# Gated linear attention with a squared-ReLU FFN: attention stages dealt into equal parts of FFN groups of four blocks, products of one shape kept together, loads issued from two queues

## The chip, the core and the metric

The kernel runs on one core of one Trainium2 chip. Its engines have a queue each and run side by side: TensorE (PE: matmuls; PEld: the loading of their stationary operand), VectorE (DVE), ScalarE (ACT), GpSimd (POOL) and SyncE (SP), which issues transfers. The metric is the device time of one execution in microseconds, as the median of several runs.

## What is computed

For each of 4 batches and 8 heads of width 48, over 768 positions, a state of 48 x 48 decays by alpha per row and takes up the outer product of k and v; q reads it. The result, 3072 tokens of 384, goes through an FFN with a hidden width of 2048. The weights of the FFN come as 64-bit floats, all else as 32-bit.

```python
for t in range(S):
    state = alpha[:, :, t, :, None] * state + np.einsum('bhd,bhe->bhde', k[:, :, t], v[:, :, t])
    y[:, :, t] = np.einsum('bhd,bhde->bhe', q[:, :, t], state)
...
h = np.maximum(x @ w_in, 0.0)
return (h * h @ w_out).astype(np.float32)
```

## The kernel before

A block is one batch and one chunk of 128 positions, all eight heads; block n is chunk n // 4 of batch n % 4, so there are 24, and the first four (chunk 0) have no state yet. Two heads make a pair: each head has 64 partitions, 48 of its own and 16 of padding. A block passes four stages:

- `decays` (line 190): alpha is turned on PE (aT), ACT takes Ln (la), DVE adds up along the chunk (the scan of line 195), ACT takes two Exp (b and inv).
- `turn` (206): q and k are turned on PE and scaled by b and inv on DVE.
- `scores` (215): sc, the products of k and q, two heads side by side in the rows of the array; DVE copies their causal part to am (226); k is turned back (kr) and copied by ACT to ks, but not in the last chunk.
- `values` (238): kv, the new part of the state (250), added by DVE in sm (259 or 261) and decayed by POOL (278); then y. For each of four pairs of heads y takes a full product with the old state (267, all 128 columns of the array; not at chunk 0) and two column-half ones, one for each head, of am with v (271). ACT copies y to yg and to xT. Heads have 48 rows and the FFN wants 128 full ones, so the fourth pair's rows fill the padding of the other three: six DMAs from yg to xT on SP (291).

The FFN works on groups of blocks, GROUPS = [2, 2, 4, 4, 4, 4, 4]. `ffn_in(g, j)` (299) makes 128 of the hidden rows for all columns of the group (h, three matmuls, 512 columns for four blocks), ACT's relu (r, line 313) and DVE's square (hid, line 314); `ffn_out(g, t, i)` (318) adds an eighth of the hidden rows to block t's output (o), and at the last eighth copies it and sends it out. A 32-bit matmul shows as two MATMUL instructions in the trace, a transpose as one. h and r have two buffers each.

The weights come in 16 pieces, eight of w_in and then eight of w_out, 768 KB each. `load_weights` (99) brings a piece to a raw buffer, of which there are two; a w_in piece takes four DMAs, all on SP. `convert_weights` (116) makes 32-bit floats of it: one ACT operation (129), five on DVE (130 to 145), two on POOL (148, 149). `next_weights` (157) converts the next piece and starts one more load.

The order of the work is written out by hand and each engine keeps it. The loop of line 357 turns block n, takes the decays of block n + 1, the values of block n - 1 and the scores of block n, with `ffn(0.25, n)` behind each: `next_weights`, then as many FFN units as make a quarter of a block's work. A group's units are queued once the values of its last block are issued, so that its first h stands right behind that y on PE. Conversion starts with block 0.

Of the kernel before, what the change touches and what calls it, by code (L numbers as in the profile page):

```python
# [15 lines left out]
GROUPS = [2, 2, 4, 4, 4, 4, 4]  # L16
# [3 lines left out]
def kernel(  # L20
# [32 lines left out]
    assert S % C == 0 and H * D == DM and NP == KM + 1 and KM * G == D and sum(GROUPS) == NBLK  # L53
# [6 lines left out]
    p3 = ctx.enter_context(tc.tile_pool(name="p3", bufs=3))  # L60
    x_pool = ctx.enter_context(tc.tile_pool(name="x", bufs=3))
# [12 lines left out]
    tiles["v"] = kept("v_in", NV, [128, H, 64])  # L74
    for i in range(NV):
        for x, value in (("a", 1.0), ("q", 0.0), ("k", 0.0), ("v", 0.0)):
            if i < len(tiles[x]):
                nc.gpsimd.memset(tiles[x][i][:, :, D:64], value)
# [7 lines left out]
    def load(n):  # L86
        c, b = divmod(n, B)
        for x in "aqkv":
            nc.sync.dma_start(  # L89
                out=tiles[x][n % len(tiles[x])][:, :, 0:D],  # L90
                in_=srcs[x][b, :, c * C : (c + 1) * C, :].rearrange("h s d -> s h d"),
            )
# [6 lines left out]
    def load_weights(i):  # L99
        dst = (w_in + w_out)[i]  # L100
        dt = moe_w_in.dtype
        raw = dst if dt == FP32 else raw_pool.tile(list(dst.shape), dt, tag="raw", name="raw")
        raws[i] = raw
        if i < NW:
            src = moe_w_in[:, i * DF // NW : (i + 1) * DF // NW]
            own = src[0 : 2 * KM * D].rearrange("(k e r) f -> e r k f", e=2, r=D)
            gap = src[2 * KM * D : DM].rearrange("(e k r) f -> e r k f", e=2, r=G)
# [70 lines left out]
    blk_group = [(g, t) for g, m in enumerate(GROUPS) for t in range(m)]  # L178
# [11 lines left out]
    def decays(n):  # L190
        ps = turned("a", n)
        la = p2.tile([128, NP, C], FP32, tag="la", name="la")
        nc.scalar.activation(out=la, in_=ps, func=AF.Ln)  # L193

        nc.vector.tensor_tensor_scan(  # L195
            out=la.rearrange("a p t -> a (p t)"),
            data0=again.rearrange("a p t -> a (p t)"),
            data1=la.rearrange("a p t -> a (p t)"),
            initial=0.0, op0=ALU.mult, op1=ALU.add,
        )  # L200
        b = bs[n] = p3.tile([128, NP, C], FP32, tag="b", name="b")
        nc.scalar.activation(out=b, in_=la, func=AF.Exp)
        inv = invs[n] = p2.tile([128, NP, C], FP32, tag="inv", name="inv")
        nc.scalar.activation(out=inv, in_=la, func=AF.Exp, scale=-1.0)

    def turn(n):
        qkT[n] = []
        for x, factor in (("q", bs[n]), ("k", invs.pop(n))):
            ps = turned(x, n)
            t = (p3 if x == "q" else p2).tile([128, NP, C], FP32, tag=f"{x}T", name=f"{x}T")  # L210
            nc.vector.tensor_tensor(out=t, in0=ps, in1=factor, op=ALU.mult)  # L211
            qkT[n].append(t)

    def scores(n):
        qT, kT = qkT[n]
        ps = [ps_att.tile([128, NP, C], FP32, tag="att", name="sc") for _ in range(2)]
        for p in range(NP):
            for e in range(2):
                rows = slice(64 * e, 64 * e + 64)
                nc.tensor.matmul(  # L220
                    out=ps[e][:, p, :], lhsT=kT[rows, p, :], rhs=qT[rows, p, :],
                    start=True, stop=True,
                )
# [14 lines left out]
    def values(n):  # L238
# [7 lines left out]
        if c < NCH - 1:  # L246
            kv = ps_att.tile([128, NP, C], FP32, tag="att", name="kv")
            kt = ks.pop(n)
            for p in range(NP):
                nc.tensor.matmul(  # L250
                    out=kv[:, p, :], lhsT=kt[:, p, :],
                    rhs=v_in[:, 2 * p : 2 * p + 2, :].rearrange("a h d -> a (h d)"),
                    start=True, stop=True,
                )
            sm = p2.tile([128, NP, D], FP32, tag="sm", name="sm")
            for e in range(2):
                rows, cols = slice(64 * e, 64 * e + 64), slice(64 * e, 64 * e + D)
                if c == 0:
                    nc.vector.tensor_copy(out=sm[rows], in_=kv[rows, :, cols])
                else:  # L260
                    nc.vector.tensor_tensor(
                        out=sm[rows], in0=kv[rows, :, cols], in1=st[rows, :, cols], op=ALU.add
                    )
        y = ps_att.tile([128, NP, C], FP32, tag="att", name="y")
        for p in range(NP):
            if c:
                nc.tensor.matmul(  # L267
                    out=y[:, p, :], lhsT=st[:, p, :], rhs=qT[:, p, :], start=True, stop=False
                )
            for e in range(2):  # L270
                nc.tensor.matmul(  # L271
                    out=y[64 * e : 64 * e + 64, p, :], lhsT=v_in[:, 2 * p + e, :],
                    rhs=am[:, e, p, :], start=(c == 0), stop=True,
                )
        if kv is not None:
            for e in range(2):
                rows, cols = slice(64 * e, 64 * e + 64), slice(64 * e, 64 * e + D)
                nc.gpsimd.tensor_tensor(  # L278
                    out=st[rows, :, cols], in0=sm[rows],
                    in1=b[rows, :, C - 1 : C].to_broadcast([64, NP, D]), op=ALU.mult,  # L280
                )
        g, t = blk_group[n]
        if t == 0:
            xT[g] = x_pool.tile([128, KM, 512], FP32, tag="xT", name="xT")
# [14 lines left out]
    def ffn_in(g, j):  # L299
        n = GROUPS[g] * C  # L300
        hid[g, j] = hid_pool.tile([128, 512], FP32, tag="hid", name="hid")
        w, c0 = w_in[j * NW // NJ], j % (NJ // NW) * 128
        ps = ps_h.tile([128, 512], FP32, tag="h", name="h")
        for kk in range(KM):
            nc.tensor.matmul(  # L305
                out=ps[:, 0:n],
                lhsT=w[:, kk, c0 : c0 + 128],
                rhs=xT[g][:, kk, 0:n],
                start=(kk == 0),
                stop=(kk == KM - 1),  # L310
            )
        r = p2.tile([128, 512], FP32, tag="r", name="r")
        nc.scalar.activation(out=r[:, 0:n], in_=ps[:, 0:n], func=AF.Relu)  # L313
        nc.vector.tensor_tensor(  # L314
            out=hid[g, j][:, 0:n], in0=r[:, 0:n], in1=r[:, 0:n], op=ALU.mult
        )

    def ffn_out(g, t, i):
        per = NJ // NW
        if i == 0:  # L320
            acc[g, t] = ps_o.tile([128, 512], FP32, tag="o", name="o")
        ps = acc[g, t]
        for j in range(per):
            nc.tensor.matmul(  # L324
                out=ps[:, 0:DM],
                lhsT=hid[g, per * i + j][:, t * C : (t + 1) * C],
                rhs=w_out[i][:, j, :],
                start=(i == 0 and j == 0),
                stop=(i == NW - 1 and j == per - 1),
            )  # L330
        if i == NW - 1:
            o = p2.tile([128, DM], FP32, tag="osb", name="osb")
            nc.scalar.activation(out=o, in_=acc.pop((g, t))[:, 0:DM], func=AF.Copy)  # L333
            c, b = divmod(sum(GROUPS[:g]) + t, B)
# [4 lines left out]
    units = []  # L339
    behind = [0.0]  # L340

    def add_group(g):
        m = GROUPS[g]
        units.extend((KM * m * C, ffn_in, (g, j)) for j in range(NJ))
        units.extend((NJ // NW * DM, ffn_out, (g, t, i)) for t in range(m) for i in range(NW))

    def ffn(share, n):
        next_weights()
        behind[0] = behind[0] + share * C * NJ * KM * 2 if units else 0.0
        while units and behind[0] > 0:  # L350
            cost, fn, args = units.pop(0)
            behind[0] -= cost
            fn(*args)

    load(2)
    decays(0)
    for n in range(NBLK + 1):
        if n < NBLK:
            turn(n)
        ffn(0.25, n)  # L360
        if n + 1 < NBLK:
            decays(n + 1)
        ffn(0.25, n)
        if n:
            values(n - 1)
            g, t = blk_group[n - 1]
            if t == GROUPS[g] - 1:
                add_group(g)
        if n + 3 < NBLK:
            load(n + 3)  # L370
        ffn(0.25, n)
        if n < NBLK:
            scores(n)
        ffn(0.25, n)
    while units:
        _, fn, args = units.pop(0)
        fn(*args)
# [30 lines left out]
```

## Time and profile before

| | |
|---|---|
| median of 3 runs | 795.09 us (794.25 to 796.36) |
| the profiled execution | 797.68 us |
| its span | 795.9 us |
| its granted TensorE clock, mean | 0.929 |
| PE busy | 684.4 us (86%) |
| DVE busy | 262.8 us (33%) |
| ACT busy | 153.2 us (19%) |
| POOL busy | 87.5 us (11%) |
| DMA, mean over the span | 48 GB/s |

The profile is of one execution. Line numbers are those of the kernel before; tiles go by the names in the code. In the chain of work a row is a start, a length, an engine or a DMA, and what it did; rows of it say what the last instruction of the kernel was waiting for at that time. In the timelines a row is an operation, with its output, its inputs, their sizes and how many were merged, and in brackets how long the engine sat idle before it and what ended that. In the groups by line stand the busy time, the mean in nanoseconds of one, and the idle time before them with its cause.

### The profile page before, as it was taken

To read this page: it belongs to the slowest core of one execution; us is meant where nothing else is said; L and a number is where in the kernel's file an instruction comes from. 1 tells how busy PE (TensorE), PEld (TensorE's weight loads), DVE (VectorE), ACT (ScalarE), POOL (GpSimd) and SP (SyncE) were. 2 spreads that over 40 slices of the span, in tenths; PEclk is the share of its full clock that TensorE was granted. 3 is DMA by queue.
4 is the path that set the end of the run, shared out by engine and by line. 5 is a ranking of instruction groups with operands and counts; after the bars stand their busy time and mean duration, and the time that the engine had idled before them with its cause. 6 is when DMAs were issued, how large, how long until landed. Compare 5 with 4: busy or idle time off the path is not lost.

```text
span 795.9 us, 7515 instructions
## 1 busy us (share of the span) xinstructions
PE 684.4 (86%) x2896; PEld 411.7 (52%) x2896; DVE 262.8 (33%) x360; ACT 153.2 (19%) x293; POOL 87.5 (11%) x93
## 2 busy tenths in 40 slices
PE   4132487779996999997999998999989999979998
PEld 3132365467673556663456654556654456644454
DVE  5589899123141342111341112341113331002200
ACT  2121233123031231111230111220111220012100
POOL 3455634100010000000000000000000000000000
PEclk9555599889998999999999998999998999999999
DMA  9986624030235023123023203023302000000000
GB/s 155 166 141 143 154 80 82 11 53 0 53 55 82 1 42 53 25 47 43 2 41 53 50 23 43 7 36 53 52 21 41 4 2 11 23 13 1 0 21 20
DMA packets 113699, 37.85 MB, mean 48 GB/s; under 512 B 103168, under 2 KB 108544, under 8 KB 113664
## 3 DMA queue, kind: packets, MB, share of 16 engines
q1 hardware_dynamic: 113664, 37.37, 27.2%
q8 instruction: 23, 0.38, 0.2%
q14 instruction: 12, 0.10, 0.0%
HBM read 31.46 MB, written 4.72 MB: 45 GB/s over the span
## 4 chain that ended last, share of the span: by engine, by line
PE 80%; DMA 6%; DVE 6%; SPq 5%; issue 1%; ACT 1%; POOL 0%; ACTq 0%; DVEq 0%; POOLq 0%
PE h L305 32%; PE o L324 31%; PE y L271 4%; PE y L267 4%; DMA raw<-in_moe_w_in_dram 3%; PE sc L220 3%; SPq L89 2%; PE kv L250 2%; DMA xT<-yg 2%; SPq L291 1%; PE kr L234 1%; PE qT L185 1%; PE kT L185 1%; PE aT L185 1%; DVE cut L133 1%
## 5 line engine op out<-in xcount | busy, mean ns | idle before, releaser
L305 PE MATMUL h<-xT,w_in 128*128 128x512 f32 (+1 forms) x672 | 273.0, 562 | 52.7 <-DMA xT<-yg 40.6
L324 PE MATMUL o<-w_out,hid 128*128 128x384 f32 x768 | 256.9, 490 | 5.7 <-POOL w_out L149 5.7
L305 PEld LDWEIGHTS h<-xT,w_in 128*128 128x128 f32 x672 | 132.3, 203 | 168.8 <-issue 141.7
L324 PEld LDWEIGHTS o<-w_out,hid 128*128 128x128 f32 x768 | 143.3, 191 | 100.7 <-POOL w_out L149 6.8
L314 DVE TENSOR_TENSOR hid<-r 128x512 f32<-128x512 f32 (+1 forms) x112 | 78.9, 712 | 251.3 <-ACT r L313 251.3
L313 ACT ACTIVATE r<-h 128x512 f32<-128x512 f32 (+1 forms) x112 | 59.6, 534 | 233.9 <-PE h L305 222.2
L278 POOL TENSOR_TENSOR s<-sm,b 64x192 f32<-64x192 f32 x40 | 22.4, 560 | 434.2 <-PE y L267 415.3
L226 DVE COPY_PREDICATED am<-causal,sc 128x512 f32<-128x512 uint32 x48 | 32.3, 727 | 93.2 <-PE sc L220 93.0
L271 PE MATMUL y<-am,v_in 128*64 128x128 f32 x384 | 41.3, 307 | 8.3 <-DVE qT L211 8.3
L195 DVE TENSOR_TENSOR_SCAN la<-again,la 128x512 f32<-128x512 f32 x24 | 29.3, 1220 | 43.2 <-ACT la L193 43.1
L333 ACT ACTIVATE osb<-o 128x384 f32<-128x384 f32 x24 | 11.8, 490 | 141.8 <-PE o L324 130.6
L267 PE MATMUL y<-qT,s 128*128 128x128 f32 x160 | 37.0, 313 | 0.0
L220 PEld LDWEIGHTS sc<-qT,kT 64*128 64x128 f32 x384 | 25.4, 198 | 14.9 <-issue 11.6
L211 DVE TENSOR_TENSOR qT<-qT,b 128x512 f32<-128x512 f32 x24 | 16.4, 685 | 47.0 <-PE qT L185 31.5
L220 PE MATMUL sc<-qT,kT 64*128 64x128 f32 x384 | 30.5, 298 | 1.4 <-ACT la L193 1.4
L185 PE MATMUL aT<-ident,a_in 128*128 128x128 f32 x96 | 16.5, 300 | 17.5 <-DMA a_in<-in_alpha_dram 10.2
L271 PEld LDWEIGHTS y<-am,v_in 128*64 128x64 f32 x384 | 20.7, 142 | 18.8 <-DVE qT L211 8.8
L267 PEld LDWEIGHTS y<-qT,s 128*128 128x128 f32 x160 | 24.2, 189 | 11.8 <-issue 11.2
L185 PE MATMUL kT<-ident,k_in 128*128 128x128 f32 x96 | 16.1, 295 | 14.6 <-ACT ks L236 14.5
L185 PEld LDWEIGHTS aT<-ident,a_in 128*128 128x128 f32 x96 | 12.7, 154 | 25.7 <-DVE am L226 8.1
L250 PEld LDWEIGHTS kv<-v_in,ks 128*128 128x128 f32 x160 | 22.4, 206 | 5.1 <-DVE hid L314 1.4
L193 ACT ACTIVATE la<-aT 128x512 f32<-128x512 f32 x24 | 14.3, 595 | 54.3 <-PE aT L185 54.3
(42 smaller groups left out, 343.0 us busy)
## 6 DMA issues: line engine op xcount, KB each, us to landing
raw<-in_moe_w_out_dram SPq DMA_DIRECT2D x8, 768.0 KB, 4.5
a_in<-in_alpha_dram SPq DMA_DIRECT2D x24, 192.0 KB, 3.4
q_in<-in_q_dram SPq DMA_DIRECT2D x24, 192.0 KB, 3.9
k_in<-in_k_dram SPq DMA_DIRECT2D x24, 192.0 KB, 4.5
v_in<-in_v_dram SPq DMA_DIRECT2D x24, 192.0 KB, 4.7
raw<-in_moe_w_in_dram SPq DMA_DIRECT2D x16, 288.0 KB, 6.4
out_dram<-osb SPq DMA_DIRECT2D x24, 192.0 KB, 1.9
xT<-yg SPq DMA_DIRECT2D x144, 8.0 KB, 1.7
```

The source lines that it names most:

```text
L185: nc.tensor.transpose(out=ps[:, p, :], in_=rows[:, 128 * p : 128 * (p + 1)], identity=ident)
L195: nc.vector.tensor_tensor_scan(out=la.rearrange("a p t -> a (p t)"), data0=again.rearrange("a p t -> a (p t)"), data1=la.rearrange("a p t ...
L220: nc.tensor.matmul(out=ps[e][:, p, :], lhsT=kT[rows, p, :], rhs=qT[rows, p, :], start=True, stop=True,)
L226: nc.vector.copy_predicated(out=am_t[n % NAM][:, e], mask=causal.bitcast(U32).unsqueeze(1).to_broadcast([128, NP, C]), data=ps[e],)
L250: nc.tensor.matmul(out=kv[:, p, :], lhsT=kt[:, p, :], rhs=v_in[:, 2 * p : 2 * p + 2, :].rearrange("a h d -> a (h d)"), start=True, stop=True,)
L267: nc.tensor.matmul(out=y[:, p, :], lhsT=st[:, p, :], rhs=qT[:, p, :], start=True, stop=False)
L271: nc.tensor.matmul(out=y[64 * e : 64 * e + 64, p, :], lhsT=v_in[:, 2 * p + e, :], rhs=am[:, e, p, :], start=(c == 0), stop=True,)
L278: nc.gpsimd.tensor_tensor(out=st[rows, :, cols], in0=sm[rows], in1=b[rows, :, C - 1 : C].to_broadcast([64, NP, D]), op=ALU.mult,)
L305: nc.tensor.matmul(out=ps[:, 0:n], lhsT=w[:, kk, c0 : c0 + 128], rhs=xT[g][:, kk, 0:n], start=(kk == 0), stop=(kk == KM - 1),)
L313: nc.scalar.activation(out=r[:, 0:n], in_=ps[:, 0:n], func=AF.Relu)
L314: nc.vector.tensor_tensor(out=hid[g, j][:, 0:n], in0=r[:, 0:n], in1=r[:, 0:n], op=ALU.mult)
L324: nc.tensor.matmul(out=ps[:, 0:DM], lhsT=hid[g, per * i + j][:, t * C : (t + 1) * C], rhs=w_out[i][:, j, :], start=(i == 0 and j == 0), st ...
```

## The change

The groups are six of four blocks (GB = 4). Before the first FFN unit all four blocks of the first group pass their attention stages; then a group's FFN is cut into 16 equal slots, and ahead of each slot stands one stage of a block of the next group: slot 0 decays of its first block, slot 1 turn, slot 2 scores, slot 3 values, and so on to slot 15. A slot holds two `ffn_in` (slots 0 to 7) or four `ffn_out`. Conversion begins with block 3, three pieces before slot 0, then one piece in even slots and two in odd ones. Inputs of three blocks are loaded at the start, ahead of all weights; there are three raw buffers; the lower half of each w_in piece is loaded by SP and the upper half by ACT. In y all full products come first and all column-half ones after them. v lies without padding, so that kv has 96 columns instead of 128 and sc, sm and the decay of the state use 48 rows for a head instead of 64. b, q's and xT's tiles lose a buffer each.

```diff
-GROUPS = [2, 2, 4, 4, 4, 4, 4]
+GB = 4
...
-    raw_pool = ctx.enter_context(tc.tile_pool(name="raw", bufs=2))
+    raw_pool = ctx.enter_context(tc.tile_pool(name="raw", bufs=NR))
...
-    p3 = ctx.enter_context(tc.tile_pool(name="p3", bufs=3))
-    x_pool = ctx.enter_context(tc.tile_pool(name="x", bufs=3))
+    x_pool = ctx.enter_context(tc.tile_pool(name="x", bufs=2))
...
+    tiles["v"] = kept("v_in", NV, [128, H * D + G])
...
-            for e in range(2):
-                nc.sync.dma_start(out=raw[64 * e : 64 * e + D], in_=own[e])
-                nc.sync.dma_start(out=raw[64 * e + D : 64 * e + 64], in_=gap[e])
+            for e, dma in enumerate((nc.sync, nc.scalar)):
+                dma.dma_start(out=raw[64 * e : 64 * e + D], in_=own[:, e])
+                dma.dma_start(out=raw[64 * e + D : 64 * e + 64], in_=gap[:, e])
...
-    load(0)
-    load_weights(0)
-    load(1)
-    load_weights(1)
-    to_load, to_convert = list(range(2, 2 * NW)), list(range(2 * NW))
+    for n in range(NIN):
+        load(n)
+    to_load, to_convert = list(range(2 * NW)), list(range(2 * NW))
...
-                rows = slice(64 * e, 64 * e + 64)
+                rows = slice(64 * e, 64 * e + D)
...
-                    rhs=v_in[:, 2 * p : 2 * p + 2, :].rearrange("a h d -> a (h d)"),
-                    start=True, stop=True,
+                    rhs=v_in[:, 2 * p * D : 2 * (p + 1) * D], start=True, stop=True,
...
+        if c:
+            for p in range(NP):
+                nc.tensor.matmul(
+                    out=y[:, p, :], lhsT=st[:, p, :], rhs=qT[:, p, :],
+                    start=(p == 0), stop=False, skip_group_check=True,
+                )
         for p in range(NP):
-            if c:
-                nc.tensor.matmul(
-                    out=y[:, p, :], lhsT=st[:, p, :], rhs=qT[:, p, :], start=True, stop=False
-                )
             for e in range(2):
                 nc.tensor.matmul(
-                    out=y[64 * e : 64 * e + 64, p, :], lhsT=v_in[:, 2 * p + e, :],
-                    rhs=am[:, e, p, :], start=(c == 0), stop=True,
+                    out=y[64 * e : 64 * e + 64, p, :], lhsT=v_in[:, (2 * p + e) * D : (2 * p + e) * D + 64],
+                    rhs=am[:, e, p, :], start=(c == 0 and p == 0), stop=True,
+                    skip_group_check=True,
                 )
...
+    stages = [decays, turn, scores, values]
+    order = [(0, 0), (0, 1), (1, 0), (0, 2), (1, 1)]
+    for n in range(2, GB):
+        order += [(n - 2, 3), (n, 0), (n - 1, 2), (n, 1)]
+    order += [(GB - 2, 3), (GB - 1, 2), (GB - 1, 3)]
+    for n, s in order:
+        stages[s](n)
+        if s == 1 and n + NIN < GB:
+            load(n + NIN)
+            for _ in range(2):
+                load_weights(to_load.pop(0))
+        if s == 3 and n + NV == GB:
+            load(n + NV)
+            load_weights(to_load.pop(0))
+        if n == GB - 1 and s > 0:
+            next_weights()
+
+    NS = GB * len(stages)
+    for g in range(NBLK // GB):
+        units = [(ffn_in, (g, j)) for j in range(NJ)]
+        units += [(ffn_out, (g, t, i)) for t in range(GB) for i in range(NW)]
+        cost = {ffn_in: KM * GB * C, ffn_out: NJ // NW * DM}
+        total = sum(cost[f] for f, _ in units)
+        done = 0
+        for slot in range(NS):
+            i, s = divmod(slot, len(stages))
+            n = (g + 1) * GB + i
+            if n < NBLK:
+                stages[s](n)
+            for _ in range(1 + s % 2):
+                next_weights()
+            if s == 0 and n + 1 < NBLK:
+                load(n + 1)
+            while units and done * NS < total * (slot + 1):
+                f, args = units.pop(0)
+                f(*args)
+                done += cost[f]
```

PE before, around the end of a group of four: o belongs to the group that ends, h to the next, kv and y to the block whose columns complete it.

```order
L324 MATMUL o<-w_out_136,hid 128x384 x2
L250 MATMUL kv<-v_in_99,ks 128x128 x4
L267 MATMUL y<-qT,s_116 128x128
L271 MATMUL y<-am_170,v_in_99 64x128 x2
L267 MATMUL y<-qT,s_116 128x128
L271 MATMUL y<-am_170,v_in_99 64x128 x2
L267 MATMUL y<-qT,s_116 128x128
L271 MATMUL y<-am_170,v_in_99 64x128 x2
L267 MATMUL y<-qT,s_116 128x128
L271 MATMUL y<-am_170,v_in_99 64x128 x2
L305 MATMUL h<-xT,w_in_121 128x512 x6
L220 MATMUL sc<-qT,kT 128x128 x8
```

PE in the changed kernel, at the same place.

```order
L251 MATMUL kv<-v_in_105,ks 128x96 x4
L269 MATMUL y<-qT,s_113 128x128 x4
L275 MATMUL y<-am_161,v_in_105 64x128 x8
L322 MATMUL o<-w_out_130,hid 128x384 x2
L322 MATMUL o<-w_out_131,hid 128x384 x2
L322 MATMUL o<-w_out_132,hid 128x384 x2
L322 MATMUL o<-w_out_133,hid 128x384 x2
L186 MATMUL aT<-ident,a_in_84 128x128 x4
L309 MATMUL h<-xT,w_in_118 128x512 x6
```

The full and the half products of y no longer alternate, and a portion of the old group's o and the next block's aT now stand between the last y and the first h.

DVE before, near its start: the two scaled turns of block 0, the conversion of the first piece (raw, mag, cut), the scan of block 1, and the next conversion.

```order
L211 TENSOR_TENSOR qT<-qT,b 128x512
L211 TENSOR_TENSOR kT<-kT,inv 128x512
L130 TENSOR_SCALAR mag<-raw 128x768
L133 TENSOR_SCALAR cut<-raw 128x768
L137 SCALAR_TENSOR_TENSOR cut<-raw,cut 128x768
L141 SCALAR_TENSOR_TENSOR cut<-mag,cut 128x768
L145 TENSOR_SCALAR mag<-cut 128x768
L195 SCALAR_TENSOR_TENSOR la<-again,la 128x512
L130 TENSOR_SCALAR mag<-raw 128x768
L133 TENSOR_SCALAR cut<-raw 128x768
```

DVE in the changed kernel, from the scan of block 3 to its first conversion.

```order
L196 SCALAR_TENSOR_TENSOR la<-again,la 128x512
L227 COPY_PREDICATED am_160<-causal,sc 128x512 x2
L212 TENSOR_TENSOR qT<-qT,b 128x512
L212 TENSOR_TENSOR kT<-kT,inv 128x512
L134 TENSOR_SCALAR mag<-raw 128x768
L137 TENSOR_SCALAR cut<-raw 128x768
L141 SCALAR_TENSOR_TENSOR cut<-raw,cut 128x768
L145 SCALAR_TENSOR_TENSOR cut<-mag,cut 128x768
L149 TENSOR_SCALAR mag<-cut 128x768
L260 COPY sm<-kv 48x192 x2
L227 COPY_PREDICATED am_161<-causal,sc 128x512 x2
```

The first conversion has moved behind the scaled turns of block 3; sixteen conversions follow, the last of them in slot 8.

More of the change, by code (lines that the diff above doesn't have):

```diff
@@ L73 @@
     tiles = {x: kept(f"{x}_in", NIN, [128, H, 64]) for x in "aqk"}
[L74 to L78, printed above, removed]
+    for i in range(NIN):
+        for x, value in (("a", 1.0), ("q", 0.0), ("k", 0.0)):
+            nc.gpsimd.memset(tiles[x][i][:, :, D:64], value)
+    tiles["v"] = kept("v_in", NV, [128, H * D + G])
+    for t in tiles["v"]:
+        nc.gpsimd.memset(t[:, H * D :], 0.0)
     s_t = kept("s", B, [128, NP, 128])
@@ L320, in ffn_out @@
         if i == 0:
-            acc[g, t] = ps_o.tile([128, 512], FP32, tag="o", name="o")
-        ps = acc[g, t]
-        for j in range(per):
+            acc[t] = ps_o.tile([128, 512], FP32, tag="o", name="o")
+        for j in range(per * i, per * (i + 1)):
             nc.tensor.matmul(
[L325 to L329, printed above, removed]
+                out=acc[t][:, 0:DM],
+                lhsT=hid[j][:, t * C : (t + 1) * C],
+                rhs=w_out[i][:, j % per, :],
+                start=(j == 0), stop=(j == NJ - 1),
             )
@@ L332, in ffn_out @@
             o = p2.tile([128, DM], FP32, tag="osb", name="osb")
-            nc.scalar.activation(out=o, in_=acc.pop((g, t))[:, 0:DM], func=AF.Copy)
-            c, b = divmod(sum(GROUPS[:g]) + t, B)
+            nc.scalar.activation(out=o, in_=acc.pop(t)[:, 0:DM], func=AF.Copy)
+            c, b = divmod(g * GB + t, B)
             r0 = (b * NCH + c) * C
             nc.sync.dma_start(out=out[r0 : r0 + C, :], in_=o)
[L339 to L374, printed above, removed]
```

57 lines of the change are left out of this document (25 added, 32 removed).

## The prediction

> **What bounds the kernel now.** I read the busy shares in 40 slices first, then the windows, then the chain of work in order of time, and last the timelines of DVE and POOL in the first 150 us. In the slices each digit is a tenth of TensorE (PE) busy in 19.9 us:
>
> ```profile
> PE   4132487779996999997999998999989999979998
> ```
>
> There are two kernels here. For some 160 us PE is mostly idle; from then on it is full but for a dip at regular places. What an edit is worth is read separately for the full part, for the dips and for the start.
>
> The full part, from the chain (start, us, engine, tile, line): one block's attention between quarter-portions of the FFN, at a sequence chunk that has a state.
>
> ```profile
> 404.77 0.44 PE qT L185 x4
> 405.21 0.44 PE kT L185 x4
> ...
> 410.80 0.44 PE aT L185 x4
> 411.23 5.15 PE h L305 x12
> 416.38 0.89 PE kv L250 x8
> 417.28 0.22 PE y L267 x2
> 417.50 0.37 PE y L271 x4
> 417.87 0.42 PE y L267 x2
> ...
> 420.23 5.36 PE o L324 x16
> 425.59 1.09 PE sc L220 x16
> 426.68 0.59 PE kr L234 x4
> ```
>
> Every piece is PE and each begins where the last one ended, so here a microsecond of PE is a microsecond of the kernel. y goes 0.22 + 0.37 and then three times 0.42 + 0.37: 2.96 us. The portion behind a y takes 0.2 more than another. Attention of a block: 3 x 0.44 + 1.09 + 0.59 + 0.89 + 2.96 + 0.2 = 7.05 us. At chunk 0 there is no full product, and y is
>
> ```profile
> 126.58 1.02 PE y L271 x16
> ```
>
> which makes 5.11 us; in the last chunk kv and kr are missing, 5.57. All 24 blocks: 4 x 5.11 + 16 x 7.05 + 4 x 5.57 = 155 us.
>
> The dips and the tail, from the chain again (first and last of the five boundaries between groups of 512 columns), and the group of h at that width:
>
> ```profile
> 245.74 7.82 PE h L305 x12
> ...
> 708.40 42.94 PE h L305 x96
> 751.34 41.30 PE o L324 x128
> 792.70 0.49 ACT osb L333
> ```
>
> ```profile
> L305 PE MATMUL h<-xT,w_in 128*128 128x512 f32 x480 | 223.0, 618 | 24.1 <-DMA xT<-yg 24.1
> ```
>
> Before the first h of a group PE waits for the DMA that brings yg into the last block's columns of xT: 24.1 us over five boundaries, 4.8 each. After it the first portions are slow: 7.82 instead of 5.15 (2.7 more) at the first, 42.94 instead of 8 x 5.15 = 41.2 (1.7) at the last; with 2.2 on average that is 11 us. So the dips cost 35 us. A group of four blocks is 41.2 + 41.3 = 82.5 us of FFN, six groups 495. After the last matmul 3.2 us remain (795.9 - 792.7).
>
> What is left is the start: 795.9 - 155 - 495 - 35 - 3.2 = 108 us of PE idle or at half clock. Two windows of it (length, then busy of PE, PEld, DVE, ACT, POOL, then granted clock, DMA share and GB/s):
>
> ```profile
> 20.00:40.00 20.00, 3.94 (x16) 3.25 (x16) 11.59 (x15) 3.24 (x4) 8.30 (x5) 0.57 1.30 166
> 60.00:80.00 20.00, 5.04 (x30) 4.11 (x28) 19.66 (x19) 2.31 (x3) 11.91 (x8) 0.50 0.68 147
> ```
>
> At first the transfers are the limit (share 1.30), later VectorE (DVE), 19.66 of 20 us. It converts the weights, together with GpSimd (POOL):
>
> ```profile
> 50.79 2.11 DVE L130 TENSOR_SCALAR mag<-raw 128x768 uint32<-128x768 uint32 x1
> 52.82 2.16 DVE L133 TENSOR_SCALAR cut<-raw 128x768 uint32<-128x768 uint32 x1
> ...
> 101.81 0.54 DVE L130 TENSOR_SCALAR mag<-raw 128x768 uint32<-128x768 uint32 x1
> ...
> 105.31 4.68 DVE L314 TENSOR_TENSOR hid<-r 128x256 f32<-128x256 f32 x4
> ```
>
> ```profile
> 105.54 1.87 POOL L148 TENSOR_TENSOR w_out<-w_out,mag 128x768 f32<-128x768 f32 x1 [7.11 <-DVE mag L145]
> 107.49 1.88 POOL L149 TENSOR_TENSOR w_out<-w_out,cut 128x768 f32<-128x768 f32 x1
> ```
>
> ```profile
> 142.49 1.81 POOL w_out L149
> ```
>
> A conversion alone takes DVE 3.5 us (101.81 to 105.31). POOL then works 3.8 us on the same piece, and next to that DVE crawls: the next conversion's first two operations take 2.1 us each where one takes 0.54 alone, and four hid of 256 columns take 4.68. The last conversion ends at 144.3, and o cannot be completed before.
>
> **The change part by part.**
>
> *y.* Eight full instructions in a row and then sixteen column-half ones. Full ones without a change of shape cost 0.22 per pair (417.28, behind kv); sixteen halves together 1.02 (chunk 0, also behind kv). So 4 x 0.22 + 1.02 = 1.90 instead of 2.96, less 1.06 on 20 blocks: -21 us. Bounds: nothing, if the change of shape is not what costs; I take the rows, since both halves of the new order stand in the trace as they are.
>
> *kv* moves 96 columns instead of 128. 512 columns take 429 ns (5.15/12), 384 take 323 (41.3/128), 128 take 111 (0.89/8): in proportion to the columns, so 83 ns, -0.22 on 20 blocks, -4 us; 0 if the weight load bounds it. The 48-row sc and sm change no column count: nothing. Dense PE work: 650 - 25 = 625 us.
>
> *Boundaries.* values of a group's last block is now in slot 15, with that slot's portion of o (5.16) and the next aT (0.44) behind it on PE before h. The wait of 4.8 is covered by 5.6, so the dip and the slow restart after it go: -35 us. In the last group no aT follows, cover 5.16. The six xT DMAs stand on SP ahead of the next load, which is issued in slot 0. Without the cover all 35 come back. x_pool, b and qT lose a buffer: blocks no longer overlap on PE, and the portions in between (5 us) hide the release.
>
> *Groups of four only.* The columns of the FFN are the same; nothing.
>
> *Start.* Now four blocks' attention precedes the first FFN. Transfers: a block's inputs or a piece of weights is 768 KB,
>
> ```profile
> raw<-in_moe_w_out_dram SPq DMA_DIRECT2D x8, 768.0 KB, 4.5
> ```
>
> at 166 GB/s 4.8 us. Half of each w_in piece is issued by ACT. Its triggers for the first two pieces stand ahead of the Ln (la) of block 1, those of the third ahead of the Ln of block 2, and a trigger that has to wait for an earlier transfer holds ACT and all behind it. The third's second trigger needs the second piece landed: 4 blocks and 2 pieces, 6 x 4.8 = 29 us. So block 2 goes on at about 30. What an attention chain takes at half clock:
>
> ```profile
> 4.00 1.09 PE L185 MATMUL aT<-ident,a_in 128*128 128x128 f32 x4 [4.00 <-DMA a_in<-in_alpha_dram]
> ```
>
> ```profile
> 8.28 0.68 DVE L211 TENSOR_TENSOR kT<-kT,inv 128x512 f32<-128x512 f32 x1
> ```
>
> 5 us from a to the scaled k, and some 2 us until the next aT has passed the kv and y in front of it: two blocks, 14 us. The first conversion then begins at 44 (before, at 13). What a trigger costs ACT no row shows; SP's cost from 0.4 to
>
> ```profile
> 7.14 4.67 SPq L89
> ```
>
> and I take the short end, since the waits are counted already; the long end on three is +13.
>
> From 44 on DVE sets the pace. Conversions 0 to 2 with the rest of blocks 2 and 3 take some 20 us (3.5 + 3.5 + 6 and 6 of attention): conversion 3 at 64. Then slots 0 to 7 hold one or two conversions each in turn, two hid and one attention step. A hid of 512 columns:
>
> ```profile
> L314 DVE TENSOR_TENSOR hid<-r 128x512 f32<-128x512 f32 x80 | 55.4, 692 | 225.3 <-ACT r L313 225.3
> L226 DVE COPY_PREDICATED am<-causal,sc 128x512 f32<-128x512 uint32 x48 | 32.3, 727 | 93.2 <-PE sc L220 93.0
> L195 DVE TENSOR_TENSOR_SCAN la<-again,la 128x512 f32<-128x512 f32 x24 | 29.3, 1220 | 43.2 <-ACT la L193 43.1
> ```
>
> 0.7 alone, and 3 to 4.4 for the two beside POOL (the four of half the width took 4.68). A pair of slots: 3.5 + 3.5 + 6 (the one behind another, 2.1 + 2.1 in front) + two times 3.7 + two steps of 1.2 (a scan; two am 1.5, two scaled turns 1.4, two sm less) = 22.8 us; four pairs 91; then slot 8's scan and conversion (4.7) and POOL (3.8): w_out is whole at 64 + 91 + 8.5 = 164 us, between 157 (hid at 3) and 172. That is 20 us later than now, but far more is done by then: attention of blocks 0 to 3 (4 x 4.9), of 4 and 5 (11.6), the transposes of 6 (1.3), and ten portions less one unit, 50: 82 us of dense work, where PE itself needs only 6.7 us per slot of 11. The start costs 164 - 82 = 82 us instead of 108: -26. PE will have been idle and starts slow once more: +2.
>
> *Two load queues.* The DMA share of 1.30 over 20 to 40 us says that the transfers, not their issue, fill the time, so I give them nothing. The Trainium skill ("DMA: Bandwidth & Descriptors", Issuing engines are not separate DMA queues) says that queues of several engines run on the same 16 DMA engines and that issuing from several only saves sequencer time; by that rule, too, the term is 0, and the ACT waits above are the price. If it were wrong and the first six transfers took half the time, the start would be shorter by up to 14 us.
>
> Sum: span 625 + 82 + 2 + 3 = 712 us. The profiled execution took 797.68 at a span of 795.9, 1.8 more: 714. It is 2.6 above the median of the runs (795.09): **712 us**.
>
> **The rivals.**
>
> *The boundaries stay.* If SP or ACT is late at slot 15 by over a microsecond (5.6 of cover against 4.8), a wait and with it a slow restart come back; in full 712 + 35 = 747. Against: the queues are nearly empty in the full part. 0.08.
>
> *y gains nothing*: 712 + 21 = 733. For it: no row has the two shapes in separate blocks with a state. 0.07.
>
> *A late start.* ACT's triggers take the long end, or the conversions stretch to 12 us: w_out at 180, 728 us. 0.12.
>
> *A short start.* hid and steps slip between POOL's spans, or transfers gain from the second queue: w_out at 146, 694 us. 0.12.
>
> *Lockstep, slower than before.* In slots 0 to 9, h waits for r's release by hid, hid stands behind this slot's conversions, and ACT's relu behind ACT's wait for DVE. If PE could not work ahead over the two h and two r buffers, a slot would be DVE's 11.4 plus PE's 6.7, at half clock 13.4: 25 us, ten slots 250 from 64 on, w_out's end at 314 and 862 us. From 20 us per slot on it would be slower than before. Against: the weights come three conversions ahead, and only slots 0 and 1 hold ACT triggers that wait for DVE. 0.03.
>
> **How the numbers follow.** The forecast holds 0.58, with 704 (hid at 3 us) to 722 (w_out at 172 and two rests of 1 us) as its own range. To hold 8 in 10 the range takes in the short and the late start and stops at y without gain: 692 to 734. A change under 0.3% (2.4 us), about what a measurement of this kernel can tell from none, would need a loss of 83 us that meets the gain exactly: 0.01. Slower is the lockstep, 0.03; faster 0.96.
>
> **What would show it.** Right: y of a block with a state in two pieces of 0.9 and 1.0 us; kv at 0.67; no wait of h for xT<-yg after 250 us; PE between 170 us and the end in one piece; the first conversion at about 44 and POOL's last at about 164. Wrong: conversions spaced 12 us or more, ACT idle beyond 35 us on a DMA, h waiting at group starts, or y in one block at 3 us.

## The result, and the profile after

The changed kernel takes **723.51 us** (median of 4 runs, 721.67 to 723.62), beside 795.08 us (794.25 to 796.36) of the kernel before on the same chip: a ratio of 0.9093, with a 95% interval of 0.9074 to 0.9112. The forecast was 712 us, with a range of 692 to 734; the narrower range of the forecast alone, 704 to 722, was just missed. The profiled execution took 723.61 us at a span of 721.8.

The busy tenths of PE in 40 slices (18 us each), and the clock that TensorE was granted:

```profile
PE   4685765867999999999999999999999999999998
PEclk9877996985999999999999999999999999999999
```

The dips at the group boundaries are gone: from the eleventh slice on PE is full and at full clock. The kernel has only two parts left, a start of some 170 us and a dense rest. One boundary between groups, from the chain (start, us, engine, tile, line):

```profile
207.09 0.86 PE kv L251 x8
207.95 0.92 PE y L269 x8
208.87 1.02 PE y L275 x16
209.90 5.36 PE o L322 x16
215.25 0.44 PE aT L186 x4
215.69 5.15 PE h L309 x12
```

y takes 0.92 + 1.02 = 1.94 us where it took 2.96, and 5.36 + 0.44 of work stands between the last y and the first h, which then takes its 5.15 at once. kv takes 0.86 and not the 0.67 that was forecast.

The five largest sums of PE's waits (total, times, longest):

```profile
PE h L309 <- ACT r L314: 15.7, 2, 14.1
PE o L322 <- POOL w_out L153: 11.5, 3, 5.5
PE qT L186 <- ACT la L194: 9.7, 2, 6.9
PE h L309 <- DMA xT<-yg: 8.0, 1, 8.0
PE aT L186 <- DMA a_in<-in_alpha_dram: 5.0, 2, 3.9
```

The wait of h for xT<-yg was 24.1 us over five boundaries; it stands once, ahead of the very first h. The rest belongs to the start. There, from the timelines of DVE and ACT, the first conversion, conversion 3, and the Ln of blocks 1 and 2:

```profile
43.87 0.56 DVE L134 TENSOR_SCALAR mag<-raw 128x768 uint32<-128x768 uint32 x1
...
63.60 2.12 DVE L134 TENSOR_SCALAR mag<-raw 128x768 uint32<-128x768 uint32 x1
```

```profile
18.70 0.60 ACT L194 ACTIVATE la<-aT 128x512 f32<-128x512 f32 x1 [10.60 <-DMA k_in<-in_k_dram]
...
30.89 0.60 ACT L194 ACTIVATE la<-aT 128x512 f32<-128x512 f32 x1 [3.99 <-DMA raw<-in_moe_w_in_dram]
```

Neither Ln reads what the bracket names. ACT's triggers for the weights stand ahead of them, and these wait for earlier transfers. From 44 us on DVE sets the pace, as forecast (length, then busy of PE, PEld, DVE, ACT, POOL, clock, DMA share, GB/s), while in the dense part DVE is busy for only 118.5 of 460 us:

```profile
60.00:80.00 20.00, 16.66 (x54) 7.95 (x55) 19.67 (x20) 6.54 (x11) 11.51 (x6) 0.81 0.81 140
100.00:120.00 20.00, 5.92 (x16) 2.91 (x15) 19.73 (x18) 4.51 (x7) 11.48 (x6) 0.63 0.41 128
180.00:640.00 460.00, 460.00 (x2060) 273.66 (x2059) 118.50 (x178) 95.16 (x184) 14.25 (x28) 1.00 0.21 38
```

The end of the start, from the chain: POOL's last step of the last piece, and what PE does once it may go on.

```profile
165.71 1.81 POOL w_out L153
...
167.57 2.93 PE o L322 x4
170.49 2.01 PE sc L221 x16
172.50 1.04 PE kr L235 x4
173.54 6.90 PE o L322 x16
180.44 0.86 PE kv L251 x8
```

w_out is whole at 167.5 (144.3 before), and the first four rows take 12.9 us; at full clock the same pieces take 1.29 + 1.09 + 0.59 + 5.16 = 8.13. After a wait of 5.5 us PE runs slow for 13 us (the tenth slice, 162 to 180 us, shows 5 tenths of the clock), and that costs 4.75.

### The profile page after: what moved, and what is told of

It reads as the page before. It is cut to its first block, busy times and chain, and to the rows that moved or that the text cites. A ratio compares the mean times of both kernels' runs of the same rounds, so it can differ in the third digit from the quotient of the medians.

```text
span 721.8 us, 7282 instructions
## 1 busy us (share of the span) xinstructions
PE 659.7 (91%) x2800; PEld 387.0 (54%) x2800; DVE 268.7 (37%) x344; ACT 149.5 (21%) x277; POOL 92.3 (13%) x93
## 4 chain that ended last, share of the span: by engine, by line
PE 79%; DVE 13%; SPq 3%; DMA 3%; issue 1%; POOL 1%; ACT 0%; ACTq 0%; DVEq 0%; POOLq 0%
PE o L322 34%; PE h L309 30%; PE sc L221 3%; PE y L275 3%; DVE hid L315 3%; DVE cut L141 2%; SPq L93 2%; PE y L269 2%; PE kv L251 2%; DVE cut L145 2%; DMA raw<-in_moe_w_in_dram 2%; DVE cut L137 2%; PE kT L186 1%; DVE mag L134 1%; PE kr L235 1%
## 5 line engine op out<-in xcount | busy, mean ns | idle before, releaser
L309 PE MATMUL h<-xT,w_in 128*128 128x512 f32 x576 | 262.4, 608 | 23.7 <-ACT r L314 15.7
L309 PEld LDWEIGHTS h<-xT,w_in 128*128 128x128 f32 x576 | 108.6, 195 | 149.7 <-issue 139.0
L315 DVE TENSOR_TENSOR hid<-r 128x512 f32<-128x512 f32 x96 | 78.5, 825 | 176.0 <-ACT r L314 175.9
L314 ACT ACTIVATE r<-h 128x512 f32<-128x512 f32 x96 | 56.8, 595 | 177.6 <-PE h L309 158.3
L283 POOL TENSOR_TENSOR s<-sm,b 48x192 f32<-48x192 f32 x40 | 23.3, 581 | 381.0 <-PE y L269 346.8
L221 PEld LDWEIGHTS sc<-qT,kT 48*128 48x128 f32 x384 | 25.4, 202 | 14.6 <-issue 13.1
L221 PE MATMUL sc<-qT,kT 48*128 48x128 f32 x384 | 30.2, 300 | 0.0
L262 DVE TENSOR_TENSOR sm<-kv,s 48x192 f32<-48x192 f32 x32 | 11.3, 353 | 45.3 <-PE kv L251 44.8
L203 ACT ACTIVATE b<-la 128x512 f32<-128x512 f32 x24 | 15.1, 630 | 62.6 <-DVE la L196 62.6
L251 PEld LDWEIGHTS kv<-v_in,ks 128*128 128x128 f32 x160 | 22.3, 205 | 8.0 <-issue 3.8
L186 PE MATMUL qT<-ident,q_in 128*128 128x128 f32 x96 | 15.9, 292 | 9.7 <-ACT la L194 9.7
L251 PE MATMUL kv<-v_in,ks 128*128 128x96 f32 x160 | 22.7, 289 | 1.0 <-ACT ks L237 1.0
L186 PEld LDWEIGHTS qT<-ident,q_in 128*128 128x128 f32 x96 | 12.6, 150 | 19.1 <-ACT la L194 10.3
```

Source lines behind the costliest of these rows:

```text
L186: nc.tensor.transpose(out=ps[:, p, :], in_=rows[:, 128 * p : 128 * (p + 1)], identity=ident)
L221: nc.tensor.matmul(out=ps[e][:, p, :], lhsT=kT[rows, p, :], rhs=qT[rows, p, :], start=True, stop=True,)
L251: nc.tensor.matmul(out=kv[:, p, :], lhsT=kt[:, p, :], rhs=v_in[:, 2 * p * D : 2 * (p + 1) * D], start=True, stop=True,)
L283: nc.gpsimd.tensor_tensor(out=st[rows, :, 64 * e : 64 * e + D], in0=sm[rows], in1=b[rows, :, C - 1 : C].to_broadcast([D, NP, D]), op=ALU.mult,
L309: nc.tensor.matmul(out=ps, lhsT=w[:, kk, c0 : c0 + 128], rhs=xT[g][:, kk, :], start=(kk == 0), stop=(kk == KM - 1),)
L314: nc.scalar.activation(out=r, in_=ps, func=AF.Relu)
```

## The experiments

Theory: dense PE time has become shorter by y's order, the boundary dips are covered by the stage that stands ahead of its portion, and the start is bound by DVE next to POOL. Each run was taken beside the kernel before on its chip, and its ratio is to that one.

| run | median us (range) | ratio (95%) |
|---|---|---|
| before, y grouped | 775.92 (775.26 to 776.99) | 0.975 (0.9733 to 0.9766) |
| after, y alternating | 739.66 (738.96 to 742.06) | 0.9295 (0.9276 to 0.9314) |
| after, stage behind its portion | 754.57 (754.27 to 755.26) | 0.9478 (0.9464 to 0.9492) |
| after, one load queue | 712.27 (710.45 to 712.41) | 0.894 (0.8925 to 0.8956) |
| after, conversion on DVE alone | 712.09 (709.52 to 715.13) | 0.8958 (0.8927 to 0.899) |
| both of these | 704.38 (702.46 to 705.27) | 0.8854 (0.8828 to 0.888) |
| both, xT ahead of the loads | 702.3 (700.43 to 703.32) | 0.8821 (0.879 to 0.8853) |
| the same, four raw buffers | 700.81 (699.56 to 702.14) | 0.8811 (0.8782 to 0.884) |
| after, kv of 48 columns | 723.01 (one run) | |
| after, no conversion | 676.78 (one run) | |

### The order of y alone, in the kernel before

```diff
+        if c:
+            for p in range(NP):
+                nc.tensor.matmul(
+                    out=y[:, p, :], lhsT=st[:, p, :], rhs=qT[:, p, :],
+                    start=(p == 0), stop=False, skip_group_check=True,
+                )
         for p in range(NP):
-            if c:
-                nc.tensor.matmul(
-                    out=y[:, p, :], lhsT=st[:, p, :], rhs=qT[:, p, :], start=True, stop=False
-                )
             for e in range(2):
...
-                    rhs=am[:, e, p, :], start=(c == 0), stop=True,
+                    rhs=am[:, e, p, :], start=(c == 0 and p == 0), stop=True,
+                    skip_group_check=True,
```

> The kernel before with one part of the change: y's full products first, then its column-half ones. My theory: the change of shape between neighbours is what costs, 1.02 us per block with a state (2.96 against 1.94 in the changed kernel), 20 blocks, all on a full PE: 795.1 - 20.4, about 774 to 776. Rival (the order of y gains nothing, the gain of the whole change is all start and boundaries): 795.

795.93 became 775.92, -20.0 us. From its chain, y of a block with a state:

```profile
407.67 0.89 PE y L267 x8
408.56 1.02 PE y L273 x16
```

0.89 + 1.02 = 1.91 instead of 2.96, and 20 times 1.05 is 21. Nothing was touched but the order and the flags that mark where an accumulation starts, so the order of y is shown to cost this. That it is the change of shape shows best on the full products: behind column-half ones they took 0.42 instead of 0.22, although they write other columns than those, and o behind a y pays the same 0.2 (5.36 instead of 5.16). This is 0.6 of the 1.05. The rest lies on column-half products behind a full one that wrote the same columns, and there no run parts the shape from the columns.

### The old order of y, in the changed kernel

The loops, shown here, and the flags go back together.

```diff
-        if c:
-            for p in range(NP):
+        for p in range(NP):
+            if c:
                 ...
-        for p in range(NP):
             for e in range(2):
```

> The changed kernel with y alternating again, all else kept. My theory: 18 of the 20 blocks with a state come when PE is full (2 of them in slots 0 to 7, where DVE sets the pace and PE has time to spare), so +18 to +20 us: 741 to 744. Rival (y's part is worth less once the boundaries are covered): under 735.

+16.2 us by the medians; by the profiled executions the span went from 721.8 to 740.3, +18.5. From its chain, the first two of y's four pairs:

```profile
208.75 0.25 PE y L269 x2
209.00 0.37 PE y L273 x4
209.37 0.42 PE y L269 x2
209.79 0.37 PE y L273 x4
```

y takes 2.99 us again, 1.05 more. Of the 20 blocks with a state two pass in the start, where PE has time; 18 x 1.05 = 18.9. The medians came out 2.7 under this, the profiled executions 0.4; to that the size is right.

### The stage behind its portion

```diff
-            if n < NBLK:
-                stages[s](n)
             for _ in range(1 + s % 2):
                 next_weights()
-            if s == 0 and n + 1 < NBLK:
-                load(n + 1)
             while units and done * NS < total * (slot + 1):
                 ...
+            if n < NBLK:
+                stages[s](n)
+            if s == 0 and n + 1 < NBLK:
+                load(n + 1)
```

> The changed kernel with each slot's attention stage behind its portion of the FFN instead of ahead of it, so that the values of a group's last block stand right in front of the next group's h. My theory: the wait for xT<-yg and the slow restart come back at all five boundaries, 4.4 to 4.8 us of waiting and 2.2 of restart each, +33 to +35 us: 756 to 759. Rival (the dips went because the queues are emptier or because b, q and xT have other buffers, not because of the cover): no wait, 723.

754.57, +31. From its waits, and from its chain at the boundary:

```profile
PE h L309 <- DMA xT<-yg: 22.3, 5, 4.7
```

```profile
211.60 1.05 PE y L275 x16
...
215.18 1.75 DMA xT<-yg
...
217.28 7.97 PE h L309 x12
```

The wait is back five times, and the h behind it takes 7.97 instead of 5.15. So the dips went because of the portion that stands in front, and not by the equal slots, the groups of four, the emptier queues or the other buffers, all of which this run keeps. The first pieces of h take 2.8, 2.4, 1.9, 1.9 and 3.0 us more than at full clock, so the five boundaries cost 22.3 + 12.1 = 34.4 us, as expected. The run came out 2 to 4 us under the expectation because its start was 3.3 shorter: w_out was whole at 166.3 instead of 167.5, and the restart behind it cost 2.7 instead of 4.75.

### One load queue

```diff
-            for e, dma in enumerate((nc.sync, nc.scalar)):
+            for e, dma in enumerate((nc.sync, nc.sync)):
```

> The changed kernel with all loads of w_in on SP, none on ACT. My theory: the transfers fill the first 30 us whoever issues them, and ACT's triggers held the Ln of blocks 1 and 2 (10.6 and 4.0 us of waiting for landings), so without them the first conversion comes 6 to 11 us earlier, and as DVE sets the pace until the last conversion the end comes as much earlier: 713 to 718. Rival (the second queue speeds the loads up and is a part of the gain): 725 to 730, with the first conversion later than at 43.9.

712.27, 11.2 us less than the changed kernel: the second queue makes it slower. Its timelines of ACT, DVE and POOL:

```profile
9.63 0.60 ACT L194 ACTIVATE la<-aT 128x512 f32<-128x512 f32 x1 [1.42 <-PE aT L186]
17.80 0.60 ACT L194 ACTIVATE la<-aT 128x512 f32<-128x512 f32 x1
```

```profile
28.54 0.56 DVE L134 TENSOR_SCALAR mag<-raw 128x768 uint32<-128x768 uint32 x1
```

```profile
156.85 1.80 POOL L153 TENSOR_TENSOR w_out<-w_out,cut 128x768 f32<-128x768 f32 x1
```

Without triggers in its queue ACT goes on at 9.6 and 17.8 instead of 18.7 and 30.9; the first conversion comes 15.3 us earlier, the last 8.9 earlier, and the restart behind it costs 2.3 instead of 4.75. 8.9 + 2.4 is the 11.3 of the spans; that the 2.4 belong to the queue is not shown, since the restart also differs between other runs (under Restart, below). Of the 15.3, 6.4 are lost again on the way: SP now issues everything, and the first h waits for the six transfers of yg, which stand on SP behind loads that wait for a raw buffer; DVE has no hid to do and stands idle for 6.5 us.

```profile
PE h L309 <- DMA xT<-yg: 16.0, 1, 16.0
```

### The conversion's last two operations on DVE instead of POOL

```diff
-        nc.gpsimd.tensor_tensor(out=w, in0=w, in1=mag.bitcast(FP32), op=ALU.mult)
-        nc.gpsimd.tensor_tensor(out=w, in0=w, in1=cut.bitcast(FP32), op=ALU.add)
+        nc.vector.tensor_tensor(out=w, in0=w, in1=mag.bitcast(FP32), op=ALU.mult)
+        nc.vector.tensor_tensor(out=w, in0=w, in1=cut.bitcast(FP32), op=ALU.add)
```

> The changed kernel with the two last operations of a conversion on DVE instead of POOL. My theory: until 167 us the pace is DVE's, and half of DVE's time there is waiting beside POOL (a shift of 0.55 us takes 2.2, two hid of 1.4 take 2.9). Alone a conversion is then 3.5 + 2 x 1.04 (0.69 for 512 columns, so 1.04 for 768) = 5.6 us and a pair of slots with three of them 3 x 5.6 + 4 x 0.7 + 2.4 = 22 us against 23.3 measured: the end 4 to 8 us earlier although DVE does more, 715 to 720. Rival (DVE is slow by its own amount of work, POOL beside it costs little): 16 x 2.1 = 34 us more on the engine that sets the pace, 750 or above.

712.09, 11.4 less, where 4 to 8 were expected: the engine that bounds the start was given more work, and the start became shorter. In the profiled execution (709.52 us) w_out is whole at 156.5, 11.0 us earlier, and the restart costs 1.6 instead of 4.75. The changed kernel's DVE timeline, beside POOL's work:

```profile
78.83 2.17 DVE L137 TENSOR_SCALAR cut<-raw 128x768 uint32<-128x768 uint32 x1
81.03 2.44 DVE L141 SCALAR_TENSOR_TENSOR cut<-raw,cut 128x768 uint32<-128x768 uint32 x1
...
84.98 2.90 DVE L315 TENSOR_TENSOR hid<-r 128x512 f32<-128x512 f32 x2
...
110.70 2.81 DVE L196 TENSOR_TENSOR_SCAN la<-again,la 128x512 f32<-128x512 f32 x1
```

and this kernel's, with POOL's two operations on it:

```profile
65.05 0.55 DVE L137 TENSOR_SCALAR cut<-raw 128x768 uint32<-128x768 uint32 x1
65.63 0.96 DVE L141 SCALAR_TENSOR_TENSOR cut<-raw,cut 128x768 uint32<-128x768 uint32 x1
...
68.28 0.96 DVE L152 TENSOR_TENSOR w_in<-w_in,mag 128x768 f32<-128x768 f32 x1
69.27 0.96 DVE L153 TENSOR_TENSOR w_in<-w_in,cut 128x768 f32<-128x768 f32 x1
70.15 1.28 DVE L315 TENSOR_TENSOR hid<-r 128x512 f32<-128x512 f32 x2
...
106.61 1.22 DVE L196 TENSOR_TENSOR_SCAN la<-again,la 128x512 f32<-128x512 f32 x1
```

The two operations cost DVE 1.92 us per piece. What they had cost it from POOL is more, in the places shown: 1.6 on two hid, 1.6 on a scan, 1.6 and 1.5 on the second and third operation of a conversion that follows another. The Trainium skill ("SBUF — State Buffer", Who interferes with whom) says that DVE and GpSimd share a port pair that is an exclusive lock, and that a DVE instruction with two inputs in SBUF contends with a GpSimd instruction that reads there. The rows agree for hid, the scan and the third operation, which read two tensors from SBUF and are at their own length once POOL is idle; a scaled turn, with one input in PSUM, keeps its 0.69 us beside POOL (at 73.33 us). The second operation has one input and is stretched as well, which that sentence does not cover.

### Both together

> One load queue and the conversions wholly on DVE. My theory: the first conversion at 28.5 us as with one queue alone, and a shorter stream behind it; the two gains add up as far as the wait of the first h for xT<-yg (16 us with one queue) allows: 704 to 710. Rival (the loads become the limit once DVE is quicker): no better than with one queue alone, 712.

The edits are those of the two runs above. 704.38: 19.1 less than the changed kernel, of 22.6 if the two gains added up. What is missing is for the most part not an overlap of the two starts. In the profiled executions w_out is whole 18.4 us earlier (at 149.1), beside 8.9 + 11.0 = 19.9 for the two edits, and only these 1.5 us can lie in the wait of the first h for yg, 16.7 us here. The restart makes the larger difference: it costs 4.4 here, beside 2.3 and 1.6 with one edit alone.

### xT ahead of the loads, and then a fourth raw buffer

On top of both, the prologue only converts, and the loads that it issued follow behind the values of block 3, so that the transfers of yg pass ahead of them on SP:

```diff
-            next_weights()
+            convert_weights(to_convert.pop(0))
+    for _ in range(NR):
+        load_weights(to_load.pop(0))
```

> One queue, conversions on DVE, and in the stages before the first FFN the pieces of weights 3 to 5 are loaded after block 3's values and not between the stages of blocks 2 and 3, so that no load that waits for a raw buffer stands on SP ahead of the xT<-yg DMAs. My theory: the first h comes at 45 instead of 55.9 us and DVE, which stood still for some 4 us ahead of the first hid, goes on at once: 698 to 702. Rival (the pieces now land too late for conversions 3 to 5, and the gap only moves): 704 or more.

702.3, 2 us less, with intervals that overlap: between the two forecasts. The trace shows what the rival says: the first h waits 7.3 instead of 16.7, but the raw piece is late in turn:

```profile
55.59 0.56 DVE L134 TENSOR_SCALAR mag<-raw 128x768 uint32<-128x768 uint32 x1 [5.82 <-DMA raw<-in_moe_w_in_dram]
```

Then with one more buffer, so that a piece more is under way:

```diff
-    NR = 3
+    NR = 4
...
-            load_weights(to_load.pop(0))
+            for _ in range(2):
+                load_weights(to_load.pop(0))
...
+    for _ in range(3):
+        load_weights(to_load.pop(0))
```

> The same with four raw buffers and four pieces loaded early. My theory: if DVE's work is what sets the pace from the first conversion to the last, a piece that lands earlier changes nothing: within 2 us of the run with three. Rival (landing of pieces 3 to 5 sets the start once SP is free): 3 to 6 us faster than with three.

700.81, within 2 us as expected; the difference to the run above is inside the intervals. It is the fastest version seen, 22.7 us below the changed kernel and 94 below the one before. DVE is still the bound of its start:

```profile
100.00:120.00 20.00, 17.45 (x66) 9.19 (x68) 19.31 (x28) 6.33 (x10) 0.00 (x0) 0.84 0.67 158
```

### kv with half its columns

```diff
-            kv = ps_att.tile([128, NP, 2 * D], FP32, tag="att", name="kv")
+            kv = ps_att.tile([128, NP, D], FP32, tag="att", name="kv")
...
-                    rhs=v_in[:, 2 * p * D : 2 * (p + 1) * D], start=True, stop=True,
+                    rhs=v_in[:, 2 * p * D : (2 * p + 1) * D], start=True, stop=True,
```

> The changed kernel with kv of 48 columns instead of 96: the second head of a pair takes the first one's product, so half of the state's update is left out and the output is another. It asks why kv went from 0.89 to 0.86 us only with 96 columns instead of 128. My theory: the loading of the 128 x 128 stationary operand sets 107 ns per instruction, so kv stays at 0.86 us and the kernel at 722 to 724. Rival (the time goes with the columns above some fixed part; 128 to 96 gave 4 ns): 0.82 or less, and by the columns alone 0.36 us and 9 us off the kernel.

```profile
206.47 0.82 PE kv L251 x8
207.30 0.96 PE y L269 x8
208.26 1.02 PE y L275 x16
```

723.01, within the 722 to 724 of the theory. Half the columns again, and kv's row is 0.82 us instead of 0.86, at the rival's edge; but the full products of y behind it take 0.96 instead of 0.92. The two rows together are 0.82 + 0.96 = 1.78 us with 48 columns, 0.86 + 0.92 = 1.78 with 96 and 0.89 + 0.89 = 1.78 with 128 (the kernel before with y grouped, at 217.15 us). So the columns only move the line between the rows, and the sixteen instructions take 111 ns each whatever kv moves: the price is not that of the columns. What it is instead no run shows. The weight load is the likely one, since each instruction brings a new 128x128 operand (the group of kv's loads has a mean of 206 ns before and of 205 after), but that is argued.

### No conversion

The edit removes DVE's five operations and POOL's two from `convert_weights`.

> The changed kernel without conversions: only ACT's operation stays, DVE's five and POOL's two are left out, so the weights are wrong numbers of the same size and time of matmul. It asks what bounds the start when DVE does not. My theory: 16 pieces and seven blocks of 768 KB at 4.8 us each are landed by 110 us, and PE needs 6.7 us for each of the first ten slots from 62 us on, so PE is full from about 62 to 65 us on and slot 9 ends at 130 instead of 168: 722 - 38 - 3 of restart, 677 to 685. Rival (transfers, three raw buffers and the queues' order bound the start nearly as much as DVE): 700 or above.

676.78, 47 us less, though every transfer is made. PE in 40 slices, and its only wait of h:

```profile
PE   4684999999999999999999999999999999999998
```

```profile
PE h L287 <- DMA xT<-yg: 10.0, 1, 10.0
```

PE is full from the fifth slice on, some 70 us. The transfers of the weights, even from two queues, keep up; what fills 70 to 167 us in the changed kernel is the conversion on DVE and POOL.

## Why the prediction was right, and where it was off

**y**: right. 1.94 us (1.90 forecast), and its size holds in both kernels: -20.0 alone, +16 to +18.5 when undone. The rival that y gains nothing falls.

**Boundaries**: right. The wait is gone, PE is full, and undoing the order alone brings back 34.4 us at the boundaries, of the 35 forecast. The rival that they stay falls.

**kv**: the step that failed. "In proportion to the columns, so 83 ns" took its price from rows of 384 and 512 columns and carried it down to 96. Measured 0.86 us, 107 ns, and with the y behind it nothing saved at all: its own other bound, 0, was the answer. On the 14 such blocks that lie behind the start, 14 x 0.19 = 2.7 us.

**Start**: right in its mechanism and in its times: 44 forecast and 43.9 measured for the first conversion, 64 and 63.6 for conversion 3, 82 us of dense work by its end and 82 measured (what remains after 167.6, less restart and tail, is 721.8 - 167.6 - 4.75 - 3.2 = 546.3; less the 2.7 of kv and 0.7 of y that were too short, 542.9 of the forecast 625). The last conversion ended at 167.5, 3.5 late. So near a time is in part luck, since two errors nearly cancel: two hid beside POOL took 2.9, not 3.7, but the scan took 2.8 instead of 1.2 and the conversion's third operation 2.44 instead of 0.97, where the forecast had them at their lengths alone. From one scan to the next (62.46, 110.70 and 157.37), two pairs of slots, it is 48.2 and 46.7 us, not 45.6, and in slot 8 the scan once more. Of the 74.1 us between the spans of the two kernels about 21 are y's and 34 the boundaries'; the 19 that are left are the start's, and no run takes its parts (the order of the first blocks, the third raw buffer, the place of the conversions) back one at a time.

**Restart**: +2 forecast, 4.75 measured here. Behind the last conversion it cost 4.4 to 4.6 in four of the other runs (y alternating, kv of 48 columns, both edits together, xT ahead of the loads), 2.3 with one queue, 1.6 with the conversion on DVE and 1.8 with four raw buffers. It is not the length of the wait: 5.5 us stand ahead of the 4.75 and of the 2.3. No run here says what it is.

The span's error is then 3.5 + 2.75 + 2.7 + 0.7 (y, 0.04 on 18 blocks) = 9.7 of the 9.8 us between 712 and 721.8.

**Two load queues**: "I give them nothing" held for the transfers but left out what the other choice would have given. ACT's hold was in the sum (block 2 "at about 30", 30.9 measured), as a price that the start pays; one queue shows how large it is: w_out is whole 8.9 us earlier. The rival that transfers gain from a second queue has the wrong sign. The Trainium skill ("DMA: Bandwidth & Descriptors", Issuing engines are not separate DMA queues) has a second issuing engine save sequencer time only; the trace agrees on the transfers (157 GB/s over the first 40 us, 160 with one queue), and here the issuing engine's own work paid for it with 10.6 and 4.0 us of standing still.

**Lockstep**: there in part. PE waited 14.1 us for r once, since ACT's queue stood behind a scan that DVE had not reached. It cost nothing that the conversions didn't cost anyway: DVE was busy 19.7 of 20 us. That it made no slot longer than DVE's own work is read from this, not tried.

## What to carry to other kernels

Read every stage for its own bound, and put a stage ahead of an independent portion of the bounding engine's work if its result has to cross several engines: 5.8 us of cover took away a 4.8 us wait and the slow clock behind it. Put a load on a compute engine's queue only where its trigger finds its buffer free and its predecessors done. Before you share work between DVE and GpSimd, compare what the second engine takes off the first with what it adds to it by running beside it.

## What the runs showed of the hardware that was not expected

- Sixteen instructions of 32-bit matmuls, each with a new 128x128 stationary operand, took 1.78 us together whether eight of them moved 48, 96 or 128 columns: 111 ns each.
- A full product behind a column-half one took 0.42 us instead of 0.22.
- Beside POOL's additions and products on SBUF, not only hid but a scan (1.22 to 2.81 us) and an operation with a scalar and two tensors (0.97 to 2.44) are stretched on DVE. Without POOL's two operations the start was 11.0 us shorter, although DVE then spent 1.92 us more on each of the 16 pieces.
- DMA triggers on ACT that had to wait kept ACT idle for 10.6 and 4.0 us; aT lay ready for it during the last 9.3 and 3.8 of them.
- After 5.0 to 6.3 us of idle time PE lost from 1.6 to 4.75 us to the restart; after the same 5.5 us it lost 4.75 in one kernel and 2.3 in another.
